# Attention, forward and backward in one loop: four products of X ahead of the transposes of E, and one engine for their copies

## The chip, the cores and the metric

The kernel runs on one core of one Trainium2 chip. The metric is the device time of one execution in microseconds. The time before is 2208.2 us, the median of three runs (2205.89 to 2212.59).

A core has a matrix engine (TensorE, PE in the profile; its weight loads are listed as PEld), VectorE (DVE), ScalarE (ACT), GpSimd (POOL) and SyncE (SP), which here only issues transfers. Matrix products land in PSUM, which has eight banks of 128 x 512 f32; VectorE and ScalarE read them from there.

## The reference

A transformer block and its gradients: `s` is an attention of the normalised input, `g` a gated MLP of the same input, the output is `x + s * g`, and the kernel returns it with the gradients of seven inputs. The part that matters here is the attention, with 32 heads of 16 columns over 2048 rows, and its backward pass:

```
qkv = (x @ wqkv).reshape(B, S, 3, H, Dh)          # S = 2048, H = 32, Dh = 16
scores = einsum("bhqd,bhkd->bhqk", q, k) * Dh**-0.5
p = softmax(scores, axis=-1)
o = einsum("bhqk,bhkd->bhqd", p, v)
out = x + (o @ wo) * silu(mlp(x))                  # x normalised first
_, vjp = jax.vjp(forward, ...); grads = vjp(grad_out)
```

## The kernel before

A first part (`Pre`) normalises, projects and runs the MLP; a last part (`Grads.run`) makes the gradients of the weights and of x. Between them stands `attention_core`, which this change touches.

**Tiling.** The heads are taken in 16 pairs, the queries in 4 groups of 512: 64 blocks. A block walks over the 16 groups of 128 keys, so there are 1024 steps `g`, with `j = g // 16` the block and `kb = g % 16` the group of keys. The numbers "step 0" to "step 15" are `g % 16`.

**What a step computes**, for both heads `hj` of the pair:
- `s` (L1093): scores, keys x queries, two products of 32 rows x 512 columns; `d` (L1115): the same for grad-out times V. The four are addressed to four row groups of the array (positions 0, 32, 64, 96).
- `ets` (L1102): ScalarE's exponential of the two `s`, called E below, one instruction of 128 x 1024.
- `gts` (L1133): VectorE's two products of `d` and E.
- `tT` (L1194, L1197): PE transposes seven of the eight 128 x 128 blocks of E into one PSUM bank (`emit_T`). The eighth is left to a DMA. In steps 1 and 2 of a block only four are transposed at once (`cut`), and in six later steps an eighth transpose makes up for it (`older`, L1197). `emit_T(g - 1)` runs in step g, so in a block's own count the eight-transpose steps are 5 to 10 and the four-transpose steps 2 and 3.
- `ek`: the copy of `tT` into SBUF. ScalarE copies most of it (L1211); VectorE the eighth block (L1145).
- `X` (L1229, L1232, L1236): three groups of four products with weights of 32 or 17 columns at the four column groups of the array, each 256 columns wide; they accumulate over the 16 steps of a block: E times K and V ("e"), the row sums of E ("l"), and `gts` times K and a column of -1 ("g"). At the end of a block VectorE copies X to `xs` (L1245).
- `Z` (L1332): four products, 32 weight columns, 512 columns, for the block of 20 steps before (`ZOFF = -20`); at its ends VectorE adds Z to `acc` (L1344, L1346).
- In steps 2 and 3, `XT` (L1264): two f32 transposes of `xs`, into the free half of `tT`, copied by VectorE (L1272); POOL turns them into the weights of Z.

**What sets the order.** Nothing is scheduled: each engine does its instructions in the order in which the loop emits them. On PE in step g: d of g, two s of g + 1, d of g, T of g - 1, XT, X "e", "l", "g" of g - 1, Z. On ScalarE: exp of g + 1, then the copy of T of g - 1. On VectorE: first product of g, copies of `tT` and of XT, second product, `xs`, `acc`.

**Buffers in PSUM.** `s` has one buffer of two banks, `tT` one, `d` three, `X` one, `Z` one: all eight. So s of g + 1 waits until exp of g is done; T of g - 1 waits until `tT` of g - 2 has been copied; a `d` waits for the product that read the `d` three earlier; X's first product of a block waits for the copy of X of the block before.

**VCOPY** (L1119) is a table by step: for T of steps 12, 13 and 14 ScalarE copies six blocks of `tT` (`emit_cT(..., nc.scalar.copy)`, L1397) and VectorE the seventh, between its two products (`emit_cT` in `emit_mult`).

Of the kernel before, what the change touches and what calls it, by code (L numbers as in the profile page):

```python
# [9 lines left out]
f32 = mybir.dt.float32  # L10
# [43 lines left out]
def op_load_list(k, t, p, ld):  # L54

    L = []
    for hj in range(2):
        h = 2 * p + hj
        L.append(lambda h=h, hj=hj: ld(out=t["KVT"][32 * hj + 1:32 * hj + 17, :], in_=k.KT_s[h * 16:h * 16 + 16, :]))
        L.append(lambda h=h, hj=hj: ld(out=t["QDT"][32 * hj + 1:32 * hj + 17, :], in_=k.QT_s[h * 16:h * 16 + 16, :]))  # L60
        L.append(lambda h=h, hj=hj: ld(out=t["QDT"][32 * hj:32 * hj + 1, :], in_=k.UT_s[h:h + 1, :]))
    for hj in range(2):
        h = 2 * p + hj
        L.append(lambda h=h, hj=hj: ld(out=t["KVT"][64 + 32 * hj:80 + 32 * hj, :], in_=k.VT_s[h * 16:h * 16 + 16, :]))
        L.append(lambda h=h, hj=hj: ld(out=t["QDT"][64 + 32 * hj:80 + 32 * hj, :], in_=k.DOT_s[h * 16:h * 16 + 16, :]))
    L.append(lambda: ld(out=t["NAT"][:].rearrange("q k j c -> q k (j c)"), in_=k.NAT_s[p]))
    return L


def natq_loads(k, t, p, ld):  # L70
    return [lambda n=n, d=d: ld(out=t[n][:].rearrange("q k j c -> q k (j c)"), in_=d[p])
            for n, d in (("NATQq", k.NATQq_s), ("NATQd", k.NATQd_s))]
# [956 lines left out]
def attention_core(ctx, ctx_r, tc, k, grads, Oall, dQall, dKVT_out, ident_f32, ident_bf, npairs=16, nqc=4):  # L1029
    nc = tc.nc  # L1030
# [36 lines left out]
    st_s, st_d, st_et, st_gt, st_T = {}, {}, {}, {}, {}  # L1067
    blk = [dict(Gk={}, Ek={}) for _ in range(NB)]
    cur = {}

    def a_unit(g):
        return (g // 16, g % 16) if 0 <= g < NSTEP else None
# [6 lines left out]
    def op_of(j):  # L1079
        return OP[blocks[j][0] % 2]  # L1080
# [16 lines left out]
    def emit_exp(g):  # L1097

        a = a_unit(g)
        if a is None:  # L1100
            return
        nc.scalar.activation(out=st_et[g][:, :, :, a[1] % 4, :].rearrange("k b h q -> k h b q"),  # L1102
                             in_=cur["s"][:].rearrange("k h (b q) -> k h b q", b=4), func=ACT.Exp)
# [12 lines left out]
                         start=True, stop=True, tile_position=(r, 0))  # L1116


    VCOPY = (0, 0, 0, 0, 0, 0, 0, 0, 0, 0, 0, 0, 1, 1, 1, 0)  # L1119

    def emit_mult(g):
        a = a_unit(g)
        if a is None:
            emit_cT(g - 1, 7 - VCOPY[(g - 1) % 16], 7, nc.vector.tensor_copy)
            emit_xt(g)
            return
        kb = a[1]
        if kb % 2 == 0:
            cur["gts"] = gtp.tile([128, 2, 2, 512], bf16, name="gts")
        gts = cur["gts"]  # L1130
        st_gt[g] = gts
        for hj in range(2):
            nc.vector.tensor_tensor(out=gts[:, kb % 2, hj, :].rearrange("k (b q) -> k b q", b=4),  # L1133
                                    in0=st_d.pop((g, hj))[:].rearrange("k (b q) -> k b q", b=4),
                                    in1=st_et[g][:, :, hj, kb % 4, :], op=ALU.mult)
            if hj == 0:
                emit_cT(g - 1, 7 - VCOPY[(g - 1) % 16], 7, nc.vector.tensor_copy)
                emit_cO(g - 1)
                emit_xt(g)

    def emit_cO(g):
        if a_unit(g) is None or not older(g):
            return
        kk, i = older(g)
        nc.vector.tensor_copy(out=blk[g // 16]["Ek"][0][:, kk, i].bitcast(f32), in_=st_T[g][:, 448:512])  # L1145
# [31 lines left out]
    def cut(g):  # L1177
        return 3 if g >= 16 and g % 16 in (1, 2) else 0

    def older(g):  # L1180
        n = g % 16 - 4
        return (1 + n // 3, n % 3) if 16 <= g < NSTEP and 0 <= n < 6 else None

    def emit_T(g):
        a = a_unit(g)
        if a is None:
            return
        kk = a[1] % 4
        et = st_et[g]
        t = ps_t.tile([128, 512], f32, name="tT")  # L1190
        tb = t[:].bitcast(bf16).rearrange("q (i k) -> q i k", k=128)
        for i in range(cut(g), 7):
            b = i + a[1] // 4 % 2
            nc.tensor.transpose(tb[:, i - cut(g), :], et[:, b // 2, b % 2, kk, :], ident_bf[:])  # L1194
        if older(g):
            kk2, b = older(g)
            nc.tensor.transpose(tb[:, 7, :], st_et[g // 16 * 16 + kk2][:, b // 2, b % 2, kk2, :], ident_bf[:])  # L1197
        st_T[g] = t
        if kk == 0:
            cur["ek"] = ekc.tile([128, 4, 7, 128], bf16, name="ek")  # L1200
            blk[a[0]]["Ek"][a[1] // 4] = cur["ek"]

    def emit_cT(g, lo, hi, copy):

        a = a_unit(g)
        if a is None or lo == hi:
            return
        j, kb = a
        c = cut(g)
        lo = max(lo, c)  # L1210
        copy(out=blk[j]["Ek"][kb // 4][:, kb % 4, lo:hi].rearrange("q i k -> q (i k)").bitcast(f32),  # L1211
             in_=st_T[g][:, (lo - c) * 64:(hi - c) * 64])

    def emit_x(g, part):
        a = a_unit(g)
        if a is None:
            return
        j, kb = a
        if part == "e" and kb == 0:
            blk[j]["X"] = ps_x.tile([128, 512], f32, name="X", tag="X")  # L1220
        X = blk[j]["X"]
        NATt = op_of(j)["NAT"]
        et = st_et[g]
        for c in range(4):
            half, hj = c // 2, c % 2
            r = 32 * c
            ev = et[:, half::2, hj, kb % 4, :]
            if part == "e":
                nc.tensor.matmul(X[r:r + 32, 0:256], lhsT=NATt[:, kb, hj, 1:33], rhs=ev,  # L1229
                                 start=(kb == 0), stop=False, skip_group_check=True, tile_position=(0, r))  # L1230
            elif part == "l":
                nc.tensor.matmul(X[r:r + 32, 256:512], lhsT=Lc[:], rhs=ev,  # L1232
                                 start=False, stop=False, skip_group_check=True, tile_position=(0, r))
            else:
                gv = st_gt[g][:, kb % 2, hj, :].rearrange("k (b q) -> k b q", b=4)[:, half::2, :]
                nc.tensor.matmul(X[r:r + 17, 256:512], lhsT=NATt[:, kb, hj, 0:17], rhs=gv,  # L1236
                                 start=False, stop=(kb == 15), skip_group_check=True, tile_position=(0, r))
# [29 lines left out]
    def emit_xt(g):  # L1267
        f = fin_half(g)
        if f is None:
            return  # L1270
        j, h = f
        nc.vector.tensor_copy(out=blk[j]["xs"][:, 256 * h:256 * h + 256], in_=blk[j].pop("XT"))  # L1272
# [88 lines left out]
    for g in range(NSTEP - ZOFF):  # L1361
        cur["g"] = g
        a = a_unit(g)
        if a is not None:
            j, kb = a
            p, qc = blocks[j]
            if kb == 0 and qc == 0:
                L = natq_loads(k, k.op0, p, nc.gpsimd.dma_start) if p > 0 else []
                if p + 1 < npairs:
                    L += op_load_list(k, OP[(p + 1) % 2], p + 1, nc.gpsimd.dma_start)  # L1370
                else:
                    L += grads.tail_loads(nc.gpsimd.dma_start)
                for i, f in enumerate(L):
                    late.append((g + 16 * (i // 4) + 6 + 3 * (i % 4), f))
        emit_d(g, 0)
        emit_s(g + 1, 0)
        emit_s(g + 1, 1)
        emit_d(g, 1)
        emit_exp(g + 1)
        emit_T(g - 1)  # L1380
        emit_XT(g)
        emit_x(g - 1, "e")
        emit_x(g - 1, "l")
        emit_x(g - 1, "g")
        emit_z(g + ZOFF)
        emit_mult(g)
        emit_xs(g - 1)
        emit_fin(g)
        for it in [x for x in late if x[0] <= g]:
            late.remove(it)  # L1390

            nc.gpsimd.tensor_copy(out=tick[:], in_=st_gt[g][0:1, kb % 2, 1, 510:512])  # L1392
            it[1]()
        emit_acc(g + ZOFF)
        if g >= NSTEP:
            grads.tail_mid(g - NSTEP)
        emit_cT(g - 1, 0, 7 - VCOPY[(g - 1) % 16], nc.scalar.copy)  # L1397
        st_T.pop(g - 1, None)
        emit_dmat(g)
        st_gt.pop(g - 2, None)  # L1400
        st_et.pop(g - 12, None)
        if g == NSTEP:
            ctx_r.close()
            grads.tail_open(ps_t, ps_s, ps_d)
# [113 lines left out]
```

## Time and profile before

| | |
|---|---|
| median of three runs | 2208.2 us |
| the profiled execution | 2206.27 us |
| its span | 2204.4 us |
| mean granted TensorE clock | 0.998 |
| attention loop (first to last exponential) | 218.45 to 1858.38 us |
| in 300 to 1859 us: PE, DVE, ACT, POOL busy | 1545.5, 1457.0, 1396.0, 384.4 of 1559.0 us |

A row of the timeline has its start in us from the span's start, its duration, the engine, the source line, the operation, what it writes and reads, and how many equal neighbours are merged in it (x4); for these the duration runs to the end of the last. A bracket names what ended the idle time before it. A row of the groups has the number of instructions, the sum of their busy time and the mean of one in ns, and the engine's idle time just before them. PE's products overlap, so their durations are no distances: the time from one start to the next is what a product costs. The profile writes `128*32` for a product whose weights have 32 columns.

### The profile page before, as it was taken

The page shows a single profiled execution, that of the slowest core. Times are in us where ns is not written, and L with a number is a line of the kernel's source. Part 1 is how long each engine was busy: PE and PEld are TensorE (multiplying, and loading weights), DVE is VectorE, ACT ScalarE, POOL GpSimd, SP SyncE. Part 2 cuts the span into 40 slices and gives each one's busy share as a digit, 9 for nine tenths or more (in the row PEclk, how much of TensorE's full clock was granted, in tenths as well). Part 3 has the DMA queues.
Part 4 walks back from the last instruction along what each step waited for, and adds up shares of the span by engine and source line. Part 5 has one row for each costly group of instructions (what it writes and reads, how often), then busy time and mean ns, then how long its engine had stood idle before and what let it go on. Part 6 is the DMA issues. An engine that isn't in the chain of part 4 may idle for free.

```text
span 2204.4 us, 74272 instructions
## 1 busy us (share of the span) xinstructions
PE 2147.6 (97%) x30690; PEld 1192.5 (54%) x30690; DVE 1899.9 (86%) x3696; ACT 1758.4 (80%) x2481; POOL 590.3 (27%) x1373
## 2 busy tenths in 40 slices
PE   6999999999999999999999999999999999999998
PEld 3444555555555555555555555555555555444444
DVE  6677899999999999999999999999999998798624
ACT  5764888888888888988888989888888887784214
POOL 4276222122223222221312222222222132510002
PEclk9999999999999999999999999999999999999999
DMA  7786999999999999999999999999999999999974
GB/s 236 244 276 201 214 190 202 198 196 204 202 194 197 205 199 198 200 199 203 199 199 203 199 196 206 191 205 198 193 212 200 197 209 210 296 262 234 246 200 154
DMA packets 1422066, 461.14 MB, mean 209 GB/s; under 512 B 1334622, under 2 KB 1405918, under 8 KB 1421728
## 3 DMA queue, kind: packets, MB, share of 16 engines
q1 hardware_dynamic: 1407424, 425.46, 101.6%
q0 software_dynamic: 12720, 29.37, 4.9%
q8 instruction: 240, 3.93, 0.8%
q10 hardware_dynamic: 1584, 1.57, 0.2%
q14 instruction: 98, 0.80, 0.1%
HBM read 62.79 MB, written 64.75 MB: 58 GB/s over the span
## 4 chain that ended last, share of the span: by engine, by line
PE 90%; DVE 4%; issue 2%; ACT 2%; DMA 2%; POOL 1%; SPq 0%; DVEq 0%; ACTq 0%; POOLq 0%
PE tT L1194 24%; PE d L1115 15%; PE X L1229 10%; PE Z L1332 10%; PE X L1232 5%; PE X L1236 5%; PE ps_dw L742 2%; PE ps_dy L912 2%; PE ps_dw L984 2%; PE ps_h L352 2%; PE s L1093 2%; PE ps_m L367 2%; PE ps_dh L878 2%; PE tT L1264 1%; PE ps_dwkv L830 1%
## 5 line engine op out<-in xcount | busy, mean ns | idle before, releaser
L1133 DVE TENSOR_TENSOR gts<-d,ets 128x512 bf16<-128x512 f32 x2048 | 1366.4, 683 | 110.4 <-ACT ek L1211 46.7
L1102 ACT ACTIVATE ets<-s 128x1024 bf16<-128x1024 f32 x1024 | 1047.8, 1023 | 170.1 <-PE s L1093 82.2
L1194 PEld LDWEIGHTS <-ets 128*128 128x128 bf16 x6790 | 429.4, 97 | 248.3 <-issue 245.6
L1194 PE MATMUL tT<-ident_bf,ets 128*128 128x128 bf16 x6790 | 545.9, 219 | 14.2 <-ACT ek L1211 2.1
L1211 ACT COPY ek<-tT 128x448 f32<-128x448 f32 (+2 forms) x1024 | 510.4, 498 | 4.0 <-DVE ek L1211 1.3
L1115 PE MATMUL d<-QDT,KVT 32*128 32x512 bf16 x2048 | 450.0, 385 | 0.0
L1093 PE MATMUL s<-QDT,KVT 32*128 32x512 bf16 x2048 | 400.6, 381 | 2.6 <-ACT ets L1102 2.6
L1115 PEld LDWEIGHTS <-KVT 32*128 32x128 bf16 x2048 | 130.1, 91 | 319.2 <-issue 319.2
L1229 PE MATMUL X<-ets,NAT 128*32 128x256 bf16 x4096 | 300.5, 284 | 0.3 <-DVE xs L1245 0.3
L1236 PE MATMUL X<-gts,NAT 128*17 128x256 bf16 x4096 | 289.5, 273 | 0.0
L1232 PE MATMUL X<-ets,Lc 128*32 128x256 bf16 x4096 | 289.5, 273 | 0.0
L1392 POOL COPY tick<-gts 1x2 bf16<-1x2 bf16 x205 | 35.8, 174 | 629.7 <-DVE gts L1133 629.7
L1332 PE MATMUL Z<-gk,W 128*32 128x512 bf16 x2048 | 197.8, 379 | 1.1 <-DVE acc L1346 1.1
L1332 PE MATMUL Z<-ek,W 128*32 128x512 bf16 x1792 | 198.4, 379 | 0.0
L1229 PEld LDWEIGHTS <-NAT 128*32 128x32 bf16 x4096 | 105.9, 93 | 114.8 <-issue 21.9
L1293 POOL TENSOR_TENSOR W<-NATQq,rL 128x128 bf16<-128x128 bf16 x64 | 25.3, 396 | 503.4 <-DVE rL L1292 391.2
L1093 PEld LDWEIGHTS <-KVT 32*128 32x128 bf16 x2048 | 123.6, 91 | 8.5 <-issue 6.1
L1332 PEld LDWEIGHTS <-W 128*32 128x32 bf16 x4096 | 113.8, 97 | 11.7 <-issue 1.7
L1232 PEld LDWEIGHTS <-Lc 128*32 128x32 bf16 x4096 | 107.9, 96 | 0.0
L1236 PEld LDWEIGHTS <-NAT 128*17 128x17 bf16 x4096 | 103.4, 92 | 3.1
L1332 PE MATMUL Z<-ekd,W 128*32 128x512 bf16 x256 | 97.0, 379 | 0.0
L1197 PE MATMUL tT<-ident_bf,ets 128*128 128x128 bf16 x378 | 82.8, 219 | 0.0
(252 smaller groups left out, 2493.9 us busy)
## 6 DMA issues: line engine op xcount, KB each, us to landing
gk<-gts SPq DMA_TRANSPOSE x512, 5.3
H1T_s<-h1r SPq DMA_DIRECT2D x28, 256.0 KB, 3.9
HGT_s<-hgT SPq DMA_DIRECT2D x8, 896.0 KB, 4.4
DH_s<-stg SPq DMA_DIRECT2D x12, 512.0 KB, 3.2
hch<-DH_s SPq DMA_DIRECT2D x12, 512.0 KB, 4.4
gp<-H1T_s SPq DMA_DIRECT2D x9, 512.0 KB, 7.5
out_dram<-ob_w POOLq DMA_DIRECT2D x36, 128.0 KB, 4.6
NAT_s<-NS SPq DMA_DIRECT2D x4, 1056.0 KB, 6.2
```

The lines of the kernel that those rows point to most:

```text
L352: nc.tensor.matmul(ps[:], lhsT=w1_sb[:, ic, fc * 128:(fc + 1) * 128], rhs=yT[:, ic, g * 512:(g + 1) * 512], start=(ic == 0), stop=(ic == I ...
L1093: nc.tensor.matmul(s[:, hj, :], lhsT=op["KVT"][r:r + 32, kb * 128:(kb + 1) * 128], rhs=op["QDT"][r:r + 32, qc * 512:(qc + 1) * 512], start ...
L1102: nc.scalar.activation(out=st_et[g][:, :, :, a[1] % 4, :].rearrange("k b h q -> k h b q"), in_=cur["s"][:].rearrange("k h (b q) -> k h b q ...
L1115: nc.tensor.matmul(d[:], lhsT=op["KVT"][r:r + 32, kb * 128:(kb + 1) * 128], rhs=op["QDT"][r:r + 32, qc * 512:(qc + 1) * 512], start=True, ...
L1133: nc.vector.tensor_tensor(out=gts[:, kb % 2, hj, :].rearrange("k (b q) -> k b q", b=4), in0=st_d.pop((g, hj))[:].rearrange("k (b q) -> k b ...
L1194: nc.tensor.transpose(tb[:, i - cut(g), :], et[:, b // 2, b % 2, kk, :], ident_bf[:])
L1197: nc.tensor.transpose(tb[:, 7, :], st_et[g // 16 * 16 + kk2][:, b // 2, b % 2, kk2, :], ident_bf[:])
L1211: copy(out=blk[j]["Ek"][kb // 4][:, kb % 4, lo:hi].rearrange("q i k -> q (i k)").bitcast(f32), in_=st_T[g][:, (lo - c) * 64:(hi - c) * 64])
L1229: nc.tensor.matmul(X[r:r + 32, 0:256], lhsT=NATt[:, kb, hj, 1:33], rhs=ev, start=(kb == 0), stop=False, skip_group_check=True, tile_positi ...
L1232: nc.tensor.matmul(X[r:r + 32, 256:512], lhsT=Lc[:], rhs=ev, start=False, stop=False, skip_group_check=True, tile_position=(0, r))
L1236: nc.tensor.matmul(X[r:r + 17, 256:512], lhsT=NATt[:, kb, hj, 0:17], rhs=gv, start=False, stop=(kb == 15), skip_group_check=True, tile_pos ...
L1332: nc.tensor.matmul(Z[r:r + 32, :], lhsT=WT[j % 2][1 - part][:, qb, hj, :], rhs=mv, start=(part == 0 and qb == 0), stop=(part == 1 and qb = ...
```

## The change

Two things are changed in `attention_core`. The four "e" products of X are emitted in front of `emit_T` and `emit_XT` in all steps but step 1 of each block, where they stay behind them. And `VCOPY` is gone: `emit_cT` is called once a step, and ScalarE alone copies the seven blocks (four in steps 2 and 3) of `tT`. VectorE keeps the eighth block (`emit_cO`).

```diff
-    VCOPY = (0, 0, 0, 0, 0, 0, 0, 0, 0, 0, 0, 0, 1, 1, 1, 0)
-
     def emit_mult(g):
         a = a_unit(g)
         if a is None:
-            emit_cT(g - 1, 7 - VCOPY[(g - 1) % 16], 7, nc.vector.tensor_copy)
             emit_xt(g)
             return
...
             if hj == 0:
-                emit_cT(g - 1, 7 - VCOPY[(g - 1) % 16], 7, nc.vector.tensor_copy)
                 emit_cO(g - 1)
                 emit_xt(g)
...
-    def emit_cT(g, lo, hi, copy):
-
+    def emit_cT(g):
         a = a_unit(g)
-        if a is None or lo == hi:
+        if a is None:
             return
         j, kb = a
         c = cut(g)
-        lo = max(lo, c)
-        copy(out=blk[j]["Ek"][kb // 4][:, kb % 4, lo:hi].rearrange("q i k -> q (i k)").bitcast(f32),
-             in_=st_T[g][:, (lo - c) * 64:(hi - c) * 64])
+        nc.scalar.copy(out=blk[j]["Ek"][kb // 4][:, kb % 4, c:7].rearrange("q i k -> q (i k)").bitcast(f32),
+                       in_=st_T[g][:, 0:(7 - c) * 64])
...
         emit_exp(g + 1)
+        if g % 16 != 1:
+            emit_x(g - 1, "e")
         emit_T(g - 1)
         emit_XT(g)
-        emit_x(g - 1, "e")
+        if g % 16 == 1:
+            emit_x(g - 1, "e")
         emit_x(g - 1, "l")
         emit_x(g - 1, "g")
         emit_z(g + ZOFF)
...
-        emit_cT(g - 1, 0, 7 - VCOPY[(g - 1) % 16], nc.scalar.copy)
+        emit_cT(g - 1)
```

## The prediction

> **What bounds the kernel now.** I read the page first (span, share of each engine), then the instruction groups by line and form, then the timeline of one block of 16 steps around 1000 us.
>
> ```profile
> span 2204.4 us, 74272 instructions
> PE 2147.6 (97%) x30690; PEld 1192.5 (54%) x30690; DVE 1899.9 (86%) x3696; ACT 1758.4 (80%) x2481; POOL 590.3 (27%) x1373
> ...
> L1102 ACT ACTIVATE ets<-s 128x1024 bf16<-128x1024 f32 x1024 | 1047.8, 1023 | 170.1 <-PE s L1093 82.2 <-PE d L1115 36.4 <-ACT ek L1211 5.9
> ```
>
> There are 1024 steps, one exponential each. The first and the last start at
>
> ```profile
> 218.45 1.03 ACT L1102 ACTIVATE ets<-s 128x1024 bf16<-128x1024 f32 x1
> ...
> 1858.38 1.02 ACT L1102 ACTIVATE ets<-s 128x1024 bf16<-128x1024 f32 x1 [0.21 <-PE s L1093]
> ```
>
> so a step takes 1639.9 / 1023 = 1.603 us, and three quarters of the span is this loop. PE looks full (97%), but its rows overlap and their ends are modelled, so I read starts. Here is step 10 of a block and the head of step 11 (start, duration, engine):
>
> ```profile
> 1005.87 0.53 ACT L1211 COPY ek<-tT 128x448 f32<-128x448 f32 x1
> 1006.08 0.39 PE L1115 MATMUL d<-QDT,KVT 32*128 32x512 bf16 x1
> 1006.08 0.39 PE L1093 MATMUL s<-QDT,KVT 32*128 32x512 bf16 x2
> ...
> 1006.40 0.42 PEld L1194 LDWEIGHTS <-ets 128*128 128x128 bf16 x7 [0.23 <-issue]
> 1006.45 0.55 PE L1194 MATMUL tT<-ident_bf,ets 128*128 128x128 bf16 x7
> 1006.60 1.02 ACT L1102 ACTIVATE ets<-s 128x1024 bf16<-128x1024 f32 x1 [0.21 <-PE s L1093]
> ...
> 1006.83 0.22 PE L1197 MATMUL tT<-ident_bf,ets 128*128 128x128 bf16 x1
> ...
> 1006.98 0.29 PE L1229 MATMUL X<-ets,NAT 128*32 128x256 bf16 x4
> ...
> 1007.10 0.28 PE L1232 MATMUL X<-ets,Lc 128*32 128x256 bf16 x4
> ...
> 1007.21 0.28 PE L1236 MATMUL X<-gts,NAT 128*17 128x256 bf16 x4
> ...
> 1007.32 0.39 PE L1332 MATMUL Z<-ek,W 128*32 128x512 bf16 x4
> 1007.52 0.53 ACT L1211 COPY ek<-tT 128x448 f32<-128x448 f32 x1
> ...
> 1007.64 0.39 PE L1115 MATMUL d<-QDT,KVT 32*128 32x512 bf16 x1
> 1007.67 0.39 PE L1093 MATMUL s<-QDT,KVT 32*128 32x512 bf16 x2
> ...
> 1008.00 0.47 PEld L1194 LDWEIGHTS <-ets 128*128 128x128 bf16 x7 [0.23 <-issue]
> 1008.10 0.55 PE L1194 MATMUL tT<-ident_bf,ets 128*128 128x128 bf16 x7
> ...
> 1008.16 1.02 ACT L1102 ACTIVATE ets<-s 128x1024 bf16<-128x1024 f32 x1
> ```
>
> Three loops run side by side, with nearly one length.
> - **The copy ring.** tT has one buffer. The copy that began at 1005.87 ends at 6.40, and T starts at 1006.45; the next ends at 8.05, and T starts at 1008.10: 0.05 after the copy both times. T waits for the copy, although its weights were loaded at 6.40 and 8.00. From T to the next step's s is 1.22 us, then s to exp 0.49 to 0.52, exp to copy 0.92, copy to T 0.58: some 3.2 us for two steps, 1.6 each.
> - **The exp ring.** s has one buffer too: exp 1006.60 ends at 7.62, s starts at 1007.67, the next exp at 1008.16: 1.56 per step, whatever PE does.
> - **PE's own order.** Seven transposes lie between 1006.45 and 1006.83, so 128 columns take 0.055, 256 take 0.11 and 512 take 0.22. Whatever exceeds that is paid where the shape of the array changes: d (32 rows) to T's weights 0.32, so 0.10 extra; last T to X (32 columns) 0.15, so 0.095; Z back to d 0.32, so 0.10. X to X to Z, of one shape, pays nothing (0.12, 0.11, 0.11). A step with eight transposes is then 0.32 + 0.38 + 0.15 + 0.12 + 0.11 + 0.11 + 0.32 = 1.51 us without any wait.
>
> So PE has about 0.05 to 0.1 of wait per step, in front of T, and ScalarE's rings set the pace.
>
> **The change, part by part.** *Four X products (L1229) move between d and T in 15 of 16 steps.* Their 0.12 leaves the stretch behind T, which shortens the copy ring by 0.12 per two steps (to about 1.55 per step: no longer the bound). But they are of the 32-column shape and stand between the 32-row and the full shape, so a step changes shape four times instead of three. The one edge that has no row here is 32 rows to 32 columns. Column to full, the other new edge, is seen once behind the loop:
>
> ```profile
> 1862.07 0.38 PE L1332 MATMUL Z<-ek,W 128*32 128x512 bf16 x1
> ...
> 1862.38 0.62 PE L575 MATMUL o_tp<-ident_bf,Oall 128*128 128x128 bf16 x8
> ```
>
> 0.31 for 512 columns: 0.09 to 0.10 extra. For the unseen edge the ends are 0 (X may overlap the end of d) and 0.15 (half as much again as the dearest); I take 0.10, as all four seen edges cost that. The new step with eight transposes: d to X 0.32; X to T 0.12 + 0.10; T to second X 0.38 + 0.15; 0.12; 0.11; Z to d 0.32: 1.62 us. With seven: 1.565. Now T comes some 0.54 after d; the copy before it is done about 0.46 after d (exp at d + 0.52, copy end and wait 1.50 later, a step of 1.56 taken off). The wait is gone, and PE is the bound.
>
> The Trainium skill (TensorEngine Tiling (Array Packing), Key Properties) says that changing the tiling mode, not merely the tile, drains TensorE: a rule that speaks against this change. The three edges of the step above, 0.095 to 0.10 each, agree with it; with no such drain on the new edge the sum would be the lower end below.
>
> *ScalarE copies seven blocks in steps 13 to 15, VectorE none.*
>
> ```profile
> L1211 ACT COPY ek<-tT 128x448 f32<-128x448 f32 x706 | 372.7, 528 | 1.4 <-PE tT L1194 0.6 <-DVE ek L1145 0.4
> ...
> L1211 ACT COPY ek<-tT 128x384 f32<-128x384 f32 x192 | 90.9, 474 | 1.5 <-DVE ek L1211 1.3
> ...
> L1211 DVE COPY ek<-tT 128x64 f32<-128x64 f32 x192 | 41.2, 214 | 0.1
> ```
>
> ScalarE gains 54 ns three times a block, VectorE loses 214. I cost both at nothing: the cover of the longer copy is X in front of T (0.54 against 0.46 above). Without that cover, T would be late by 0.054 and half of it would reach the step: 3 x 0.027 x 64 = 5 us. VectorE is not waited for in those steps.
>
> *The exception.* In step 1 X's first product waits until X of the block before is copied out:
>
> ```profile
> 1017.31 0.68 DVE L1245 COPY xs<-X 128x512 f32<-128x512 f32 x1
> ```
>
> That ends at 1017.99, 0.91 after the step's d (1017.08, below). In the new place, 0.32 after d, it would hold up T by 0.6; in the old place it costs nothing new. No DMA, no queue of SP or POOL and no buffer is moved.
>
> *VectorE's lump.* In steps 2 and 3 it also copies XT, and adds acc in 3:
>
> ```profile
> 1020.31 0.39 PE L1115 MATMUL d<-QDT,KVT 32*128 32x512 bf16 x1
> ...
> 1020.88 0.39 PE L1264 MATMUL tT<-ident_f,xs 128*128 128x128 f32 x2
> ...
> 1021.41 0.41 DVE L1272 COPY xs<-tT 128x256 f32<-128x256 f32 x1
> ...
> 1022.34 0.68 DVE L1346 TENSOR_TENSOR acc<-Z,acc 128x512 f32<-128x512 f32 x1
> 1022.94 1.87 DVE L1133 TENSOR_TENSOR gts<-d,ets 128x512 bf16<-128x512 f32 x3
> ...
> 1023.67 0.37 PE L1115 MATMUL d<-QDT,KVT 32*128 32x512 bf16 x1
> ```
>
> The second d of step 5 needs the buffer that the product begun at 1022.94 frees (end 23.62, d at 23.67): 0.25 late. In step 3 the four transposes in front of XT take 0.22, so T starts at 1020.66, 0.35 behind d, and xt's copy 1.10 behind d. With X in front, T comes at 0.54 and XT with it 0.18 later, so xt's copy waits until about 1.18, and multiplication, acc and the next product follow by 0.08; step 3 is 0.07 longer, so d of step 5 is again about 0.25 late. But then it is 0.25 on a step of 1.62 with no T wait to absorb part of it: 1.87.
>
> **The sum.** The block's stretches, from the first d of each:
>
> ```profile
> 999.63 0.38 PE L1115 MATMUL d<-QDT,KVT 32*128 32x512 bf16 x1
> ...
> 1017.08 0.38 PE L1115 MATMUL d<-QDT,KVT 32*128 32x512 bf16 x1
> ...
> 1018.70 0.39 PE L1115 MATMUL d<-QDT,KVT 32*128 32x512 bf16 x1
> ...
> 1021.86 0.38 PE L1115 MATMUL d<-QDT,KVT 32*128 32x512 bf16 x1
> ...
> 1023.42 0.39 PE L1115 MATMUL d<-QDT,KVT 32*128 32x512 bf16 x1
> ...
> 1025.18 0.39 PE L1115 MATMUL d<-QDT,KVT 32*128 32x512 bf16 x1
> ```
>
> - Steps 6 to 10 (eight transposes): 1007.64 - 999.63 = 8.01 now; 5 x 1.62 = 8.10: +0.09.
> - Steps 11 to 15 and 0 (seven): 9.44 now; PE 1.565 and the exp ring 1.56 meet, and where s waits 0.03 it is 1.60; I take 1.58: 9.48, +0.04.
> - Step 1 (old order): 1.62 now, no copy wait left over from the step before: 1.57, -0.05.
> - Steps 2, 3 (four transposes and two of f32, as long as eight): 3.16 now, 3.24: +0.08.
> - Step 4: 1.56, stays at 1.56. Step 5: 1.76, becomes 1.87: +0.11.
>
> +0.27 us a block. 63 blocks run in the steady state (the first has no Z for 20 steps and is held by the exp ring): +17 us. The profiled execution took 2206.3 us (span 2204.4 and 1.9 around it), 1.9 less than the median of the runs shown: 2223 by the one, 2225 by the other. I take **2224**.
>
> **Rivals.**
> - *The new edge is cheap (faster).* If the array takes X's 32-column weights while d still streams, d to X costs 0.22, eight-transpose steps fall to 1.52 and the exp ring's 1.56 rules all but step 5: 15 x 1.56 + 1.87 = 25.3 against 25.55, -16 us: about 2190. For it: the four d and s products of one shape do overlap entirely. Against: T's weights started 0.32 after d in both steps, never earlier. It decides from an extra of 0.06 or less. The Trainium skill (TensorE: Matmul & The Clock Gate, Part 2, "Step-by-step: what each phase is for") has LDWEIGHTS pulled ahead of running matmuls if their row groups do not conflict or the background buffer is the target; by that rule the cheap edge could be true, the rows of T's weights show no such overlap across shapes.
> - *It cancels.* An edge of 0.08, 0.02 less than taken, removes 0.02 from some 13 steps of each block, all of the +0.27: 2208, within 0.3%. For it: the rows print to 0.01 and each edge is a difference of two.
> - *Dearer: PE waits more.* An edge of 0.15 makes every step 0.05 longer: 1.67 and 1.615, +0.87 a block, +55 us: 2261. A milder form, VectorE's late xt copies pushing step 5 by another 0.3, gives +19 on top: 2243. Against: VectorE gains slack from the longer steps.
> - *The copy's new length shows.* If T still waits for the copy in steps 13 to 15, the 5 us above come on top; they lie inside the range.
>
> **How the numbers follow.** Forecast as worked out, 2212 to 2240: 0.62. Cheap edge: 0.12. Cancelling: 0.13. Dearer: 0.13. About 0.3% (6.6 us) is what a measurement of this kernel tells from no change. Slower 0.62 + 0.13 = 0.75, same 0.13, faster 0.12. The range runs from 2204, in the cancelling case, to 2250, past the milder dear case; it leaves out the cheap edge and the edge of 0.15.
>
> **What would show it.** Right: X's first product starts 0.32 after d, T 0.54 after d and no longer 0.05 behind the copy's end; steps 6 to 10 near 1.62, 11 to 15 near 1.58; ScalarE's idle time in front of exp grows; the second d of step 5 still 0.25 late. Wrong: X to T nearer 0.12 than 0.22, or d to X nearer 0.22 than 0.32; T still glued to the copy; or a late DMA or VectorE wait in front of X that no row here has.

## The result, and the profile after

| | before | after |
|---|---|---|
| median | 2208.2 us (four runs, 2205.89 to 2212.59) | 2249.85 us (four runs, 2245.21 to 2253.76) |
| ratio, 95% interval | | 1.0183 [1.0167, 1.0198] |
| span of the profiled execution | 2204.4 us | 2251.9 us |
| mean granted TensorE clock | 0.998 | 0.996 |

The change makes the kernel 42 us slower, where some 17 were forecast. The page and the instruction groups of the changed kernel (same columns as before):

```profile
span 2251.9 us, 74079 instructions
PE 2206.2 (98%) x30690; PEld 1126.0 (50%) x30690; DVE 1913.8 (85%) x3504; ACT 1778.7 (79%) x2481; POOL 592.9 (26%) x1373
...
L1102 ACT ACTIVATE ets<-s 128x1024 bf16<-128x1024 f32 x1024 | 1048.7, 1024 | 172.8 <-PE s L1093 59.6 <-PE d L1115 45.4 <-DMA ekd<-ets 5.7
```

PE is busier by 59 us with as many instructions (30690); VectorE and ScalarE have nearly the work they had. That points at PE's order. The timeline of step 6 of a block, with the copy ahead of it:

```profile
1019.74 0.53 ACT L1205 COPY ek<-tT 128x448 f32<-128x448 f32 x1
...
1019.92 0.38 PE L1115 MATMUL d<-QDT,KVT 32*128 32x512 bf16 x1
...
1020.25 0.29 PE L1223 MATMUL X<-ets,NAT 128*32 128x256 bf16 x4
...
1020.47 0.39 PEld L1190 LDWEIGHTS <-ets 128*128 128x128 bf16 x7
1020.47 0.56 PE L1190 MATMUL tT<-ident_bf,ets 128*128 128x128 bf16 x7
...
1020.87 0.22 PE L1193 MATMUL tT<-ident_bf,ets 128*128 128x128 bf16 x1
...
1021.02 0.29 PE L1226 MATMUL X<-ets,Lc 128*32 128x256 bf16 x4
...
1021.14 0.28 PE L1230 MATMUL X<-gts,NAT 128*17 128x256 bf16 x4
...
1021.25 0.39 PE L1326 MATMUL Z<-gk,W 128*32 128x512 bf16 x4
...
1021.57 0.38 PE L1115 MATMUL d<-QDT,KVT 32*128 32x512 bf16 x1
```

The copy ends at 1020.27, and T starts 0.20 later, as soon as its weights begin to load: the wait for the copy is gone. No row of PE in this step names a wait. Still the step takes 1.65 us, with four changes of shape in it: d to X 0.33, X to T 0.22, last T to X 0.15, Z to d 0.32.

The block's stretches as in the prediction: here the first d of steps 5, 11, 1, 2 and 4, and of step 5 of the next block; step 6 begins at 1019.92 above.

```profile
1018.06 0.38 PE L1115 MATMUL d<-QDT,KVT 32*128 32x512 bf16 x1
...
1028.18 0.38 PE L1115 MATMUL d<-QDT,KVT 32*128 32x512 bf16 x1
...
1037.76 0.39 PE L1115 MATMUL d<-QDT,KVT 32*128 32x512 bf16 x1
...
1039.35 0.39 PE L1115 MATMUL d<-QDT,KVT 32*128 32x512 bf16 x1
...
1042.66 0.39 PE L1115 MATMUL d<-QDT,KVT 32*128 32x512 bf16 x1
...
1044.25 0.38 PE L1115 MATMUL d<-QDT,KVT 32*128 32x512 bf16 x1
```

| steps | before | forecast | after |
|---|---|---|---|
| 6 to 10 | 8.01 | 8.10 | 8.26 |
| 11 to 15 and 0 | 9.44 | 9.48 | 9.58 |
| 1 | 1.62 | 1.57 | 1.59 |
| 2 and 3 | 3.16 | 3.24 | 3.31 |
| 4 | 1.56 | 1.56 | 1.59 |
| 5 | 1.76 | 1.87 | 1.86 |
| block | 25.55 | 25.82 | 26.19 |

+0.64 us a block times 64 is 41 of the 42 us measured. The loss is in every row but that of step 1, and most of what the forecast lacks (0.26 of 0.37 us) is in the first two rows, whose steps do nothing special. Within a row it is not even: before, the steps 6 to 10 took 1.57, 1.66, 1.56, 1.66 and 1.56 us, and now each of them takes 1.65. The change brings the short steps up to the length of the long ones, which had waited for the copy.

### The profile page after: what moved, and what is told of

Its sections match the earlier page's. It is cut to its first block, busy times and chain, and to the rows that moved or that the text cites. A ratio compares the mean times of both kernels' runs of the same rounds, so it can differ in the third digit from the quotient of the medians.

```text
span 2251.9 us, 74079 instructions
## 1 busy us (share of the span) xinstructions
PE 2206.2 (98%) x30690; PEld 1126.0 (50%) x30690; DVE 1913.8 (85%) x3504; ACT 1778.7 (79%) x2481; POOL 592.9 (26%) x1373
## 3 DMA queue, kind: packets, MB, share of 16 engines
q10 hardware_dynamic: 1584, 1.57, 0.2%
## 4 chain that ended last, share of the span: by engine, by line
PE 90%; DVE 3%; DMA 2%; SPq 2%; ACT 2%; issue 1%; POOL 1%; ACTq 0%; DVEq 0%; POOLq 0%
PE tT L1190 22%; PE d L1115 15%; PE X L1223 10%; PE X L1226 10%; PE Z L1326 10%; PE X L1230 5%; PE ps_dw L742 2%; PE ps_dy L912 2%; PE ps_h L352 2%; PE ps_dw L984 2%; PE ps_m L367 2%; PE ps_dh L878 2%; PE tT L1258 1%; PE ps_qkv L210 1%; PE tT L1193 1%
## 5 line engine op out<-in xcount | busy, mean ns | idle before, releaser
L1130 DVE TENSOR_TENSOR gts<-d,ets 128x512 bf16<-128x512 f32 x2048 | 1351.2, 683 | 125.9 <-ACT ek L1205 32.2
L1102 ACT ACTIVATE ets<-s 128x1024 bf16<-128x1024 f32 x1024 | 1048.7, 1024 | 172.8 <-PE s L1093 59.6
L1190 PE MATMUL tT<-ident_bf,ets 128*128 128x128 bf16 x6790 | 557.0, 221 | 1.4
L1205 ACT COPY ek<-tT 128x448 f32<-128x448 f32 (+1 forms) x1024 | 521.7, 509 | 24.5 <-DVE xs L1266 4.0
L1190 PEld LDWEIGHTS <-ets 128*128 128x128 bf16 x6790 | 387.0, 98 | 131.1 <-issue 15.5
L1115 PE MATMUL d<-QDT,KVT 32*128 32x512 bf16 x2048 | 428.3, 385 | 0.0
L1226 PE MATMUL X<-ets,Lc 128*32 128x256 bf16 x4096 | 299.9, 282 | 0.0
L1115 PEld LDWEIGHTS <-KVT 32*128 32x128 bf16 x2048 | 109.2, 91 | 320.2 <-issue 320.2
L1093 PEld LDWEIGHTS <-KVT 32*128 32x128 bf16 x2048 | 102.2, 91 | 10.4 <-issue 8.1
L1141 DVE COPY ek<-tT 128x64 f32<-128x64 f32 x378 | 85.0, 225 | 11.3
```

The lines of the kernel that those rows point to most:

```text
L1093: nc.tensor.matmul(s[:, hj, :], lhsT=op["KVT"][r:r + 32, kb * 128:(kb + 1) * 128], rhs=op["QDT"][r:r + 32, qc * 512:(qc + 1) * 512], start ...
L1115: nc.tensor.matmul(d[:], lhsT=op["KVT"][r:r + 32, kb * 128:(kb + 1) * 128], rhs=op["QDT"][r:r + 32, qc * 512:(qc + 1) * 512], start=True, ...
L1205: nc.scalar.copy(out=blk[j]["Ek"][kb // 4][:, kb % 4, c:7].rearrange("q i k -> q (i k)").bitcast(f32), in_=st_T[g][:, 0:(7 - c) * 64])
L1226: nc.tensor.matmul(X[r:r + 32, 256:512], lhsT=Lc[:], rhs=ev, start=False, stop=False, skip_group_check=True, tile_position=(0, r))
```

## The experiments

The theory after the result: PE's own order, with one more change of shape in each step, sets the pace; the copies have nothing to do with it. The rivals: ScalarE's longer copies carry a part; or it is not the number of changes that costs but work put in front of T, since T, its copy and VectorE's copies come later by its length. Every ratio below is to the kernel before, which was run beside each version (2209.08 us in experiments 1 to 4, 2208.81 in 5 to 8); the bracket is its 95% interval.

**1. The new order alone (VCOPY kept).**

```diff
+        if g % 16 != 1:
+            emit_x(g - 1, "e")
         emit_T(g - 1)
         emit_XT(g)
-        emit_x(g - 1, "e")
+        if g % 16 == 1:
+            emit_x(g - 1, "e")
```

> The new place of X's e products, with VCOPY kept as before. Theory (PE's own order sets the pace: one more change of the array's shape a step, 1.65 us with eight transposes and 1.595 with seven): ScalarE's copies have slack, so the time is that of the changed kernel, 2250 +- 4 us, and d to X 0.315, X to T 0.216 as there. Rival (the longer copies on ScalarE in steps 13 to 15 carry part of the loss): 3 copies of 54 ns in 64 blocks give back up to 10 us, 2240 or less.

Measured: 2249.94 us, ratio 1.0181 [1.0163, 1.0198]. The whole loss is in the order.

**2. ScalarE's copies alone (the order before).** The diff of the change without its lines about `emit_x`.

> The order before, ScalarE copying all seven blocks. Theory (in the order before T starts 0.05 us behind the copy of the step before, so a copy 54 ns longer shows by about half in three steps a block): 3 x 0.027 x 64 = 3 to 5 us, 2211 to 2213. Rival (the copies are covered, or VectorE gains from three copies of 214 ns less): 2208 or less.

Measured: 2209.67 us against 2209.08 for before, ratio 1.0004 [0.9994, 1.0014]. A miss of the theory's size: the 3 to 5 us are not there (at most 3 by the interval). In the two profiles step 14 is 0.05 us longer (the median over the blocks, 1.51 and 1.56), and no other step differs by more than 0.02. So most of the three longer copies is absorbed; by what is not shown.

**3. X's l products in front of T as well.**

```diff
         if g % 16 != 1:
             emit_x(g - 1, "e")
+            emit_x(g - 1, "l")
         emit_T(g - 1)
```

(and `l` is emitted behind T in step 1 only).

> As the changed kernel, but X's l products also go in front of T: as many changes of shape a step (four), 0.11 us more work in front of T. Theory (the number of shape changes is the cost): steps of 1.65 and 1.595 as in the changed kernel, only step 5 longer by about 0.1 since VectorE's copies of tT and XT come later: 2250 to 2258 us. Rival (work in front of T is the cost, as T, its copy and VectorE's copies come later by its length): as much again as the first four products cost, 42 us: about 2292.

Measured: 2252.47 us, ratio 1.0194 [1.0179, 1.021]. Twice the work in front of T costs what the first half did. A step with eight transposes, on PE:

```profile
1027.95 0.38 PE L1115 MATMUL d<-QDT,KVT 32*128 32x512 bf16 x1
...
1028.27 0.29 PE L1223 MATMUL X<-ets,NAT 128*32 128x256 bf16 x4
1028.39 0.28 PE L1226 MATMUL X<-ets,Lc 128*32 128x256 bf16 x4
1028.61 0.56 PE L1190 MATMUL tT<-ident_bf,ets 128*128 128x128 bf16 x7
...
1029.59 0.38 PE L1115 MATMUL d<-QDT,KVT 32*128 32x512 bf16 x1
```

T starts 0.66 behind d instead of 0.55, and the step, with eight transposes, takes 1.64: as many changes of shape, the same time. For this change the rival of work in front of T falls.

**4. All of X and Z in front of T: three changes of shape, with X ahead.**

```diff
-            if hj == 0:
+            if hj == (0 if g % 16 in (1, 4, 5) else 1):
                 emit_cO(g - 1)
                 emit_xt(g)
...
-        if g % 16 != 1:
-            emit_x(g - 1, "e")
-        emit_T(g - 1)
-        emit_XT(g)
-        if g % 16 == 1:
-            emit_x(g - 1, "e")
+        first = "TZ" if g % 16 == 5 else "ZT" if g % 16 == 1 else "eT" if g % 16 == 4 else ""
+        if first == "TZ":
+            emit_T(g - 1)
+            emit_z(g + ZOFF)
+        elif first == "ZT":
+            emit_z(g + ZOFF)
+            emit_T(g - 1)
+        emit_x(g - 1, "e")
+        if first == "eT":
+            emit_T(g - 1)
         emit_x(g - 1, "l")
         emit_x(g - 1, "g")
-        emit_z(g + ZOFF)
+        if first in ("", "eT"):
+            emit_z(g + ZOFF)
+        if not first:
+            emit_T(g - 1)
+            emit_XT(g)
```

> All of X and Z in front of T (steps 1, 4 and 5 of a block apart, which have Z T X, e T l g Z and T Z X), and VectorE copies tT's eighth block and XT behind its second product instead of between the two. X's e products stand in front of T as in the changed kernel, but d, X, Z, T, d has three changes of shape, as before. Theory (the number of shape changes is the cost): steps of 1.54 to 1.59 where the order is X Z T, about 25.45 us a block against 25.55 typical before: 2200 to 2212 us. Rival (X in front of T is the cost, through T and its copy coming later; here T comes some 0.45 us later still): 2250 or more.

Measured: 2271.42 us, ratio 1.0278 [1.026, 1.0295]: the total is a miss, and the rival's number. The steps show why. First step 2 of a block, which waits for nothing:

```profile
995.45 0.38 PE L1115 MATMUL d<-QDT,KVT 32*128 32x512 bf16 x1
...
995.77 0.29 PE L1223 MATMUL X<-ets,NAT 128*32 128x256 bf16 x4
...
996.11 0.39 PE L1326 MATMUL Z<-ek,W 128*32 128x512 bf16 x4
996.43 0.40 PE L1190 MATMUL tT<-ident_bf,ets 128*128 128x128 bf16 x4
...
996.99 0.38 PE L1115 MATMUL d<-QDT,KVT 32*128 32x512 bf16 x1
```

All of X and Z stand in front of T here (XT follows it, at 996.67), and the step takes 1.54 us. The changed kernel does the same products in steps 2 and 3 in 1.655 us each (3.31 above), with one change of shape more. Then the end of step 10, step 11 and the head of step 12 (VectorE, ScalarE and PE):

```profile
1010.91 0.23 DVE L1141 COPY ek<-tT 128x64 f32<-128x64 f32 x1 [0.18 <-PE tT L1193]
1011.17 0.53 ACT L1205 COPY ek<-tT 128x448 f32<-128x448 f32 x1 [0.37 <-DVE ek L1141]
...
1011.60 1.03 ACT L1102 ACTIVATE ets<-s 128x1024 bf16<-128x1024 f32 x1
...
1012.33 0.38 PE L1115 MATMUL d<-QDT,KVT 32*128 32x512 bf16 x1
...
1012.68 0.39 PE L1093 MATMUL s<-QDT,KVT 32*128 32x512 bf16 x2
```

ScalarE's copy of tT starts only when VectorE's copy of the eighth block has ended (1011.14). In the kernel before ScalarE's copies waited 4.0 us in all, as exp was running meanwhile; with T at the end of the step the wait holds the copy back, the copy holds exp, and s comes 0.35 behind d. Steps 8, 10 and 12 take 1.83 to 1.92 us (medians of this profile). In step 4, the longest with 2.18 us, ScalarE's copy waits in the same way for VectorE's copy of XT (0.43 us, at 999.31), and T for ScalarE's copy. So the length of a step without waits goes by the number of changes of shape and not by what stands in front of T. The version as a whole is slower by late copies, which is what the rival said: T some 0.45 us later is too late for them, T 0.11 later (experiment 3) is not. What the version would take without these waits is open.

**5 and 6. Short copies, in the old order and in the new.** ScalarE copies four of the seven blocks of tT; GpSimd fills the other three with zeros. The diff is the one against the changed kernel; the version in the old order has X's e products behind T again, as in experiment 2.

```diff
+            for n in range(4):
+                if cut(g + n) == 0:
+                    nc.gpsimd.memset(cur["ek"][:, n, 4:7], 0.0)
...
-        nc.scalar.copy(out=blk[j]["Ek"][kb // 4][:, kb % 4, c:7].rearrange("q i k -> q (i k)").bitcast(f32),
-                       in_=st_T[g][:, 0:(7 - c) * 64])
+        nc.scalar.copy(out=blk[j]["Ek"][kb // 4][:, kb % 4, c:c + 4].rearrange("q i k -> q (i k)").bitcast(f32),
+                       in_=st_T[g][:, 0:4 * 64])
```

> The order before, without VCOPY, and ScalarE copies only four of the seven blocks of tT in every step (372 ns instead of 528); the other three are left out of the result (GpSimd writes zeros in their place). Theory (in the order before, T waits for the copy; without that wait the exponential's own ring of 1.56 us a step is the bound): about 25.1 us a block instead of 25.6, 0.4 x 63 = 25 us less: 2178 to 2192. Rival (T's start 0.05 us behind the copy is chance and PE's own order is the bound in both kernels): 2209 +- 4.

> The changed kernel with the same four-block copies (three of seven blocks left out of the result). Theory (in the new order PE's own order is the bound, the copy has slack): unchanged, 2250 +- 4 us, steps of 1.65 and 1.595. Rival (the copy, now begun later, is still waited for): as much less as in the old order, about 2225.

Measured: 2195.66 us in the old order, ratio 0.9935 [0.991, 0.9959]; 2247.23 us in the new, 1.0174 [1.0159, 1.019]. The signs are the theory's: a copy shorter by 0.156 us helps the old order by 13 us, and the new one not measurably (the changed kernel's interval overlaps). The size in the old order is half of what was expected. Steps 6 and 13 there, the second with the copy before it:

```profile
1046.26 0.38 PE L1115 MATMUL d<-QDT,KVT 32*128 32x512 bf16 x1
...
1046.59 0.56 PE L1190 MATMUL tT<-ident_bf,ets 128*128 128x128 bf16 x7
...
1047.14 0.29 PE L1226 MATMUL X<-ets,NAT 128*32 128x256 bf16 x4
...
1047.80 0.39 PE L1115 MATMUL d<-QDT,KVT 32*128 32x512 bf16 x1
...
1057.09 0.37 ACT L1208 COPY ek<-tT 128x256 f32<-128x256 f32 x1
1057.16 0.38 PE L1115 MATMUL d<-QDT,KVT 32*128 32x512 bf16 x1
1057.24 0.39 PE L1093 MATMUL s<-QDT,KVT 32*128 32x512 bf16 x2
...
1057.57 0.56 PE L1190 MATMUL tT<-ident_bf,ets 128*128 128x128 bf16 x7
1057.73 1.02 ACT L1102 ACTIVATE ets<-s 128x1024 bf16<-128x1024 f32 x1 [0.28 <-PE d L1115]
...
1058.72 0.38 PE L1115 MATMUL d<-QDT,KVT 32*128 32x512 bf16 x1
```

In step 13 T no longer sits 0.05 behind the copy (it ends at 1057.46), s waits for exp instead, and the step has the 1.56 us of the exp ring. Step 6 waits for neither: it is PE's old order with eight transposes and three changes of shape, and takes 1.54 us. Against the 1.65 of the changed kernel, one more change costs 0.11. Step 1, where X still waits for its copy, and step 5 with its late d keep their length. A block without a late transfer takes 25.24 us in this profile (step 5 to step 5, 1044.49 to 1069.73), 0.31 less than before, which is 20 us in 64 blocks. That the time fell by 13 only fits a second wait: exp waits for the transfer that transposes E in 11 steps here, 9.1 us in all, against 3 steps and 1.4 us before (last section). That these 7.7 us are the rest is not shown.

**7. T split by X: two more changes of shape, no more work.** Part 0 of `emit_T` is the first four transposes, part 1 the others.

```diff
-        emit_T(g - 1)
-        emit_XT(g)
-        emit_x(g - 1, "e")
+        emit_T(g - 1, 0)
+        if fin_half(g) is None:
+            emit_x(g - 1, "e")
+        emit_T(g - 1, 1)
+        emit_XT(g)
+        if fin_half(g) is not None:
+            emit_x(g - 1, "e")
```

> The order before with VCOPY, but X's e products stand between T's fourth and fifth transposes (not in steps 2 and 3): five changes of shape a step instead of three, no work added. Theory (each change of shape costs what the trace of the changed kernel shows, 0.093 from T to X and 0.109 + 0.010 from X to T): PE's own order becomes 1.51 + 0.21 = 1.72 us with eight transposes and 1.665 with seven, about 27.2 us a block, +1.6 to 1.7 x 63: 2308 to 2318. Rival (the first 0.05 to 0.1 of such a change is hidden in the wait for the copy and the second change is hidden by weights loaded early): below 2270.

Measured: 2353.85 us, ratio 1.0655 [1.0639, 1.0671]: dearer than the theory by 36 us or more, far from the rival. A step with seven transposes:

```profile
1029.98 0.38 PE L1115 MATMUL d<-QDT,KVT 32*128 32x512 bf16 x1
...
1030.32 0.38 PE L1198 MATMUL tT<-ident_bf,ets 128*128 128x128 bf16 x4
1030.64 0.29 PE L1234 MATMUL X<-ets,NAT 128*32 128x256 bf16 x4
1030.86 0.34 PE L1198 MATMUL tT<-ident_bf,ets 128*128 128x128 bf16 x3
1031.13 0.29 PE L1237 MATMUL X<-ets,Lc 128*32 128x256 bf16 x4
...
1031.68 0.39 PE L1115 MATMUL d<-QDT,KVT 32*128 32x512 bf16 x1
```

1.70 us, against 1.665 expected. That sum starts from the prediction's 1.51 us for eight transposes, and step 6 of experiment 5 shows 1.54, so an estimated 1.48 with seven. The two changes more are then 0.22, or 0.11 each. With eight transposes it is 1.82 against 1.72: there the eighth block ends late, VectorE copies it late, and ScalarE's copy waits for that:

```profile
1099.82 0.23 DVE L1145 COPY ek<-tT 128x64 f32<-128x64 f32 x1 [0.19 <-PE tT L1203]
...
1100.08 0.53 ACT L1216 COPY ek<-tT 128x448 f32<-128x448 f32 x1
...
1100.66 0.38 PE L1198 MATMUL tT<-ident_bf,ets 128*128 128x128 bf16 x4
```

The copy ends at 1100.61 and T starts 0.05 later: the copy ring is back. So the total is no clean price of a change, and the steps with seven transposes nearly are: 1.48 (estimated), 1.595 and 1.70 us with three, four and five changes.

**8. Without the exception in step 1.**

```diff
-        if g % 16 != 1:
-            emit_x(g - 1, "e")
+        emit_x(g - 1, "e")
         emit_T(g - 1)
         emit_XT(g)
-        if g % 16 == 1:
-            emit_x(g - 1, "e")
```

> The changed kernel with X's e products in front of T in step 1 of a block too. Theory (X's first product of a block waits for the copy of X of the block before, which ends 0.9 us behind the step's d; in front of T it holds T up): step 1 takes about 2.08 instead of 1.59, +0.49 x 63 = 31 us: 2275 to 2285. Rival (the copy of X is early enough, or the next steps catch up): 2250 to 2258.

Measured: 2283.61 us, ratio 1.0337 [1.0322, 1.0353], 34 us above the changed kernel. Step 1 on PE and VectorE:

```profile
1055.30 0.39 PE L1115 MATMUL d<-QDT,KVT 32*128 32x512 bf16 x1
...
1055.50 0.68 DVE L1239 COPY xs<-X 128x512 f32<-128x512 f32 x1
...
1056.23 0.29 PE L1223 MATMUL X<-ets,NAT 128*32 128x256 bf16 x4 [0.54 <-DVE xs L1239]
1056.46 0.56 PE L1190 MATMUL tT<-ident_bf,ets 128*128 128x128 bf16 x7
```

X waits for the copy that ends at 1056.18, and T behind it starts 1.16 after d, where it stands 0.55 after d in other steps: 0.61 later, and the prediction had said 0.6. The step is 0.61 longer than step 1 of the changed kernel (medians of the two profiles), 39 us in 64 blocks; why 5 of them do not reach the time is open.

## Why the prediction was right and wrong

- *T's wait for the copy ends, and PE becomes the bound:* right. T starts 0.20 behind the copy in the changed kernel, and shorter copies help the old order alone (5 and 6). Only step 1, which keeps the old order, still has T 0.05 behind the copy (1038.18 behind 1038.13).
- *One more change of shape, some 0.10 us:* right in kind and in size. Experiments 3 and 4 show that the number counts and not what stands in front, and the steps without waits differ by 0.11 (1.54 and 1.65), as in the prediction (1.51 and 1.62). The edge that had no row (32 rows to 32 columns) took 0.33 from d to X, where 0.32 was taken.
- *The length of PE's own step, 1.62 and 1.565 us:* this term of the sum failed. It is 1.65 (1019.92 to 1021.57) and 1.595 (9.58 / 6). The error was there before the new edge came in: the old order without waits is 1.54 and not 1.51 (experiment 5). Of the 0.03, 0.02 is one reading. From the first transpose to X the sum has 0.38 + 0.15 = 0.53, and it is 0.55 (1020.47 to 1021.02). The 0.38 was read off a step in which T had waited for the copy with its weights loaded. Where T does not wait, the first two transposes start 0.066 apart instead of 0.055 (medians of the traces), in the new order and in the old; the rest of the 0.02 is rounding. The profile before has such a stretch, in step 5 of a block, where T follows the late d:

```profile
1023.97 0.56 PE L1194 MATMUL tT<-ident_bf,ets 128*128 128x128 bf16 x7
...
1024.52 0.29 PE L1229 MATMUL X<-ets,NAT 128*32 128x256 bf16 x4
```

The remaining 0.01 is shared by d to X and X to T (medians 0.325 and 0.226, for 0.32 and 0.22). In the kernel before, the error did no harm, as the rings set the pace there; in the new order PE's own length is the time. The prediction had itself worked out that 0.02 a step is as much as the whole forecast, and took the sum all the same.
- *The exp ring of 1.56 hides PE in the seven-transpose steps (1.58 and 1.56 taken for 11 to 15, 0 and 4):* wrong for the same reason. At 1.595 PE lies above the ring in all of them, so no step is left to absorb anything. Together the two terms are nearly all of the 0.37 us that the table's block has above its forecast (26.19 - 25.82), 24 us in 64 blocks, which with the forecast's 17 is 41 of the 42 measured.
- *The range, 2204 to 2250 us:* the measured 2249.85 lies in it by luck. Its upper end was set for VectorE's late copies of XT in step 5, and step 5 took no more than was forecast.
- *Step 5:* 1.86 for 1.87, by two errors that cancel. The second d is 0.23 late (1018.29) and not 0.25, on a step of 1.65 and not 1.62.
- *ScalarE's longer copies cost nothing:* right in the new order (1). In the old order, where half a copy's lengthening had been feared, they cost at most 3 us (2).
- *The exception:* right, T would come 0.61 later (8).
- *ScalarE's idle time in front of exp grows:* wrong place. It went from 170.1 to 172.8 us only; the group of its copies shows the rest:

```profile
L1205 ACT COPY ek<-tT 128x448 f32<-128x448 f32 (+1 forms) x1024 | 521.7, 509 | 24.5 <-DVE xs L1266 4.0
```

24.5 us idle in front of the copies, where the old kernel's group had 4.0.
- *The rivals.* A cheap new edge did not occur: X starts 0.33 behind d, and T's weights at 1020.47, 0.22 behind X's start. The Trainium skill (TensorE: Matmul & The Clock Gate, Part 2, "Step-by-step: what each phase is for") has weights pulled ahead of running products under either of two conditions, and by that rule the edge could have been cheap. These rows show no pull-ahead across shapes. "Dearer" is what came, though not through one edge of 0.15 but through 0.03 in the step. (That rival's own terms, 1.67 and 1.615, add up to 0.94 us a block and not 0.87.)

## What to carry to other kernels

Where products of several shapes alternate on TensorE, count the changes of shape in the loop before moving anything: here each costs about 0.1 us, as much as four packed products of 256 columns, and filling a wait of 0.05 to 0.1 us by work that adds one is a loss. When several rings of a loop are within a few per cent of each other, a forecast needs PE's length without waits to 0.01 us over the whole step, so read it off stretches that do not wait (step 5 of a block here) instead of adding rounded pieces from steps that do. And look at which of two readers of a PSUM bank comes first before moving a transpose: in experiment 4 ScalarE's copy started only when VectorE's had ended.

## What the runs showed of the hardware that was not expected

- A row of transposes that had to wait with its weights loaded runs a little faster than one that did not: 0.38 us from the first to the eighth in the prediction's step 10, 0.40 in step 6 of the changed kernel (1020.47 to 1020.87).
- Leaving the 32-column shape for T costs a little more than entering it: from X's second group to T 0.22 in experiment 3, where such a group takes 0.11, so 0.11 extra, against 0.15 - 0.055 = 0.095 from T to X. The difference is near the last printed digit.
- ScalarE's copy of a PSUM bank waits for VectorE's copy of another part of the same bank (0.37 us and, for the copy of XT, 0.43 us in experiment 4). This is a wait in the program, set by the order in which the two are emitted, and not shown to be one of the memory.
- The exponential sometimes waits for a transfer that transposes E (`ekd<-ets` in its row above): 5.7 us in all in the changed kernel's profile, in 9 steps, 1.4 us in 3 steps before and 9.1 us in 11 steps in experiment 5. What makes that transfer late in some steps and not in others is open.
